# Lightning attention and a highway FFN: three early loads issued from ACT's queue instead of SP's

## The chip, the cores and the metric

The kernel runs as one program on one core of a Trainium2 chip. The metric is the device time of one execution in microseconds (us), and a kernel's time is the median of its runs.

The engines are named as the profile names them: PE (matrix multiply), DVE (vector), ACT (scalar, activations), POOL (GpSimd) and SP, which in this kernel only issues DMAs. A DMA is issued by an instruction in the queue of an engine, in that engine's order. "SPq" and "ACTq" in the profile are such instructions.

## The reference

Inputs are q, k and v of shape (4, 8, 768, 64), that is batch, heads, tokens and head size, a decay `lam` per head, two 512x512 weights and a bias. All are float32.

```python
for b in range(nb):                       # blocks of 64 tokens
    intra = einsum(qb, kb) * Dmask        # Dmask[i,j] = lam**(i-j) for i >= j, else 0
    intra = einsum(intra, vb)
    inter = einsum(qb * lam_pow, kv_state)
    out[:, :, sl] = intra + inter
    kv_state = lam_block * kv_state + einsum(kb * rev_pow, vb)
x = out as (3072 tokens, 512)
H = relu(x @ w_h);  T = sigmoid(x @ w_t + b_t)
result = T * H + (1 - T) * x
```

## The kernel before

**Tiling.** The 4 batches of 768 tokens are cut into 12 steps of 256 tokens, numbered n = 0 to 11, three steps to a batch. Within a step there are two sub-blocks of 128 tokens. The decay is folded into the operands: queries are multiplied by powers of `lam` and values by the inverse powers, so that the state is a plain sum over a batch and the mask is one triangle. Keys are only cast to bfloat16.

**A written-out order.** Each engine runs its instructions in the order of the string `PLAN` (lines 17 to 64). Each word is one piece of work: a name, indices, `@` an engine where there is a choice, and `=` the buffer slots that it opens. The words that matter here, with n the step and p the half of the heads (0: heads 0 to 3, 1: heads 4 to 7, 2: all):

- `Lk.n.p`, `Lq.n.p`, `Lv.n.p` (line 179): load 256 KB of keys, queries or values as 128 partitions x 4 heads x 512 B. `W.w.g` (line 185) loads half of a weight, 512 KB.
- `CK`, `CQ`, `CV` (lines 193 to 207): cast the keys, scale the queries, scale the values, into bfloat16 tiles `kb`, `qb`, `vs`. `WC` (line 189) casts a part of a weight.
- `TK`, `TQ` (line 212): PE transposes. `EK`, `EQ` (line 219): copies of the transposes to SBUF, `kq`.
- `SA.n`, `SB.n` (lines 258 and 263): PE's scores of a step and the updates of its state. `KE` copies the state. `M.n.e.u` (line 278): DVE multiplies 128x512 of scores by the triangle, four times a step.
- `I`, `A`: PE's products with the state and with the values. `D`: copies of the attention's result to `xT`.
- `F.g.u.w` (line 327): PE's FFN products (w = 0: w_h, 1: w_t). `H`, `G`, `X`: DVE's relu, ACT's sigmoid and the product of the two. `R`: PE turns the result back, `E` copies it out, `ST` stores it.
- `Z.r` (line 404): r matrix products of zeros into an unused bank, put where PE would stand idle.
- `LB` (line 389): the powers of the factors, `pow_q` and `pow_v`, on PE, ACT and DVE.

**What sets the order of the loads.** All loads and stores are issued from SP, in the order of `PLAN`. The first ones are `Lv.0.1 Lq.0.1 Lq.0.0 Lk.1.1 Lk.1.0 Lk.0.0 Lk.0.1 Lv.0.0 Lq.1.0 Lv.1.1 Lq.1.1 W.0.1 Lv.1.0 W.0.0`, and then the queries, keys and values of step 2. ACT issues two small DMAs of its own at the very start, `lam` and the bias.

**Semaphores of DMAs.** In the built program the DMAs use eight completion semaphores in turn. A DMA that takes a semaphore which another DMA has used waits, on the engine that issues it, until that other DMA has landed. The first eight DMAs (lam, bias and six loads) wait for nothing.

**The start of the computation.** ACT casts `CK.1.0`, `CK.0.0` and `CK.0.1`, then copies `EK.0.0`, `EK.1.0` and `EK.0.1`. Then PE can do `SA.0`. DVE scales `CQ.0.0`, copies `EQ.0.0` and `EQ.0.1`, scales `CV.0.0` and `CQ.1.0`, and then masks the scores of step 0. POOL does `CV.0.1`, `CK.1.1`, `CQ.0.1`, `CV.1.1`, `CQ.1.1`, parts of the weights, and then the casts of step 2 and later (`CQ.2.2`, `CK.2.2`, `CV.2.2`, ...), each in its order.

Of the kernel before, what the change touches and what calls it, by code (L numbers as in the profile page):

```python
# [8 lines left out]
F32 = mybir.dt.float32  # L9
# [17 lines left out]
F.0.0.0=5 I.1.1=6 Lk.4.0=4 I.1.0=1 Lk.4.1 M.1.1.1=6 M.1.0.1=7 A.1.1 A.1.0 D.1.1@ACT=1 D.1.0@DVE Lv.4.1=4 B=3 Lv.4.0
KE.1.1@DVE=3 BC TQ.2.2=4 EQ.2.2@DVE=2 H.0.1=0 H.0.0=1 Lq.5.0=0 TK.2.2=2 F.1.1.0=1 EK.2.2@ACT CK.3.2@POOL=1 F.1.0.0=6
WC.1.1.0@DVE SA.2=342 SB.2=0 Lq.5.1 WC.1.1.1@ACT F.1.1.1=5 Lk.5.1=0 PT Lk.5.0 M.2.1.1=0 M.2.1.0=3 KE.2.0@ACT=0 I.2.1=2
M.2.0.1=1 G.1.1 Lv.5.0=0 F.0.1.1=4 F.1.0.1=0 G.1.0 Lv.5.1 H.1.1=2 F.0.0.1=1 X.1.1@DVE=0 Lq.6.0=1 I.2.0=5 A.2.1  # L30
M.2.0.0=2 A.2.0 G.0.1 H.1.0=2 X.1.0@DVE X.0.1@DVE=1 D.2.1@DVE=2 R.1=36 TQ.3.2=0 G.0.0 D.2.0@ACT X.0.0@DVE Lk.6.1=1
Lk.6.0 EQ.3.2@DVE=0 Lq.6.1 TK.3.2=4 F.2.1.0=2 CV.3.2@POOL=3 E.1.1@ACT=0 Lq.7.0=2 R.0=56 Lv.6.1=1 EK.3.2@ACT H.2.1=2
SA.3=104 E.0.0@DVE=1 E.0.1@ACT CQ.4.2@POOL=1 F.2.1.1=2 F.2.0.0=6 KE.3.0@ACT=2 I.3.1=5 M.3.1.1=6 SB.3=4 M.3.0.0=7
M.3.1.0=4 Lv.6.0 G.2.1 A.3.0=1 Lq.7.1 E.1.0@ACT KE.3.1@ACT=1 Lk.7.0=2 H.2.0=0 CK.4.2@POOL=0 TK.4.2=0 CV.4.2@POOL=0
EK.4.2@ACT=1 M.3.0.1=5 CQ.5.2@POOL=2 TQ.4.2=3 X.2.1@DVE=0 A.3.1 CK.5.2@POOL=2 F.2.0.1=6 EQ.4.2@DVE I.4.0=4 D.3.0@ACT=1
D.3.1@ACT SA.4=203 M.4.1.0=0 M.4.1.1=1 F.3.0.0=1 F.3.1.0=5 Lk.7.1 CV.5.2@POOL=1 Lv.7.0=2 Lv.7.1 CK.6.2@POOL=1 G.2.0
KE.4.0@ACT=0 SB.4=0 M.4.0.0=2 X.2.0@DVE I.4.1=3 KE.4.1@ACT=3 TK.5.2=2 M.4.0.1=3 TQ.5.2=6 EK.5.2@ACT=2 H.3.1=1
F.3.0.1=0 A.4.0 EQ.5.2@DVE H.3.0=2 SA.5=526 M.5.1.1=4 M.5.0.0=7 CQ.6.2@POOL=0 M.5.1.0=5 A.4.1 G.3.0 D.4.0@ACT=0
F.3.1.1=1 KE.5.0@ACT=2 SB.5=6 M.5.0.1=6 CV.6.2@POOL=2 X.3.0@DVE=1 TK.6.2=4 I.5.0=5 I.5.1=2 A.5.0 A.5.1 D.4.1@ACT G.3.1
D.5.1@ACT D.5.0@DVE R.2=36 E.2.0@DVE=2 Lq.8.1=3 X.3.1@DVE TQ.6.2=0 EQ.6.2@ACT=0 F.4.3.1=5 E.2.1@DVE EK.6.2@ACT G.4.3=0  # L40
F.4.3.0=2 H.4.3=0 F.4.1.1=3 CK.7.2@ACT=0 Lq.8.0 R.3=10 E.3.1@DVE=3 SA.6=642 M.6.1.0=0 Lk.8.1=3 Lk.9.1=4 M.6.0.0=2
CQ.7.2@POOL=1 F.4.1.0=5 H.4.1=1 TQ.7.2=0 M.6.1.1=1 KE.6.0@ACT=1 E.3.0@ACT SB.6=4 Lk.8.0 EQ.7.2@ACT=1 Lk.9.0 G.4.1=1
I.6.1=1 TK.7.2=6 M.6.0.1=3 F.4.2.1=5 EK.7.2@DVE F.4.0.0=0 X.4.3@POOL=0 KE.6.1@DVE=0 G.4.2 A.6.1=2 H.4.0=2
CV.7.2@POOL=3 SA.7=346 KE.7.0@ACT=3 A.6.0 D.6.1@ACT=1 F.4.2.0=0 D.6.0@ACT M.7.1.0=5 M.7.1.1=7 CQ.8.2@POOL=2
CK.8.2@POOL=2 SB.7=4 KE.7.1@ACT=2 Lv.8.0=3 Lv.8.1 H.4.2=3 TQ.8.2=1 TK.8.2=6 M.7.0.1=4 M.7.0.0=6 EQ.8.2@DVE=2 X.4.2@DVE
EK.8.2@ACT X.4.1@POOL F.4.0.1=2 Lq.9.1=4 Lq.9.0 I.7.0=0 G.4.0 Lk.10.0=0 Lv.9.1=4 CK.9.2@POOL=1 TK.9.2=4 EK.9.2@ACT=0
X.4.0@DVE I.7.1=3 A.7.0 A.7.1 D.7.1@ACT Lv.9.0 D.7.0@DVE Lk.11.0=1 Lq.10.1=0 Lq.10.0 CV.8.2@POOL=0 Lk.10.1 ST.1
SA.8=615 M.8.1.1=1 KE.8.0@DVE=1 R.5=24 F.5.0.0=0 E.5.1@DVE=4 M.8.1.0=3 CQ.9.2@POOL=0 TQ.9.2=3 Lv.10.0=0 F.5.3.1=5
F.5.3.0=4 H.5.0=0 E.5.0@ACT CV.9.2@POOL=1 EQ.9.2@ACT SA.9=213 M.8.0.0=0 G.5.3=2 H.5.3=1 SB.8=0 M.9.1.1=2
CQ.10.2@POOL=1 R.4=56 M.9.0.0=5 Lk.11.1 KE.9.0@ACT=0 SB.9=4 Lv.10.1 F.5.1.0=3 KE.9.1@DVE=3 F.5.2.1=2 Lq.11.1=1  # L50
M.8.0.1=6 E.4.0@ACT=0 E.4.1@ACT CK.10.2@ACT=0 I.8.0=5 I.9.1=6 G.5.2 ST.3 Lv.11.1=1 Lq.11.0 M.9.0.1=4 H.5.1=3 M.9.1.0=7
F.5.2.0=0 H.5.2=2 TQ.10.2=4 EQ.10.2@ACT=1 F.5.1.1=3 G.5.1=0 CV.10.2@POOL=2 CK.11.2@POOL=2 X.5.3@POOL=1 ST.5 X.5.2@DVE
ST.4 I.8.1=1 TK.10.2=0 Lv.11.0 EK.10.2@DVE A.9.1=2 A.9.0 D.9.0@ACT=0 D.9.1@DVE A.8.1 A.8.0 SA.10=430 D.8.0@ACT
I.10.0=6 F.5.0.1=2 G.5.0 D.8.1@DVE M.10.1.1=2 M.10.1.0=4 M.10.0.0=5 F.6.2.0=5 F.6.3.1=1 X.5.0@DVE KE.10.0@DVE=2
TK.11.2=0 CQ.11.2@POOL=2 H.6.2=2 F.6.0.0=3 H.6.0=1 EK.11.2@ACT=0 TQ.11.2=4 X.5.1@POOL R.6=25 G.6.3=1 E.6.1@ACT=3
EQ.11.2@ACT E.6.0@ACT R.7=03 E.7.0@DVE=4 E.7.1@DVE SB.10=1 CV.11.2@POOL=3 F.6.3.0=5 M.10.0.1=7 H.6.3=0 KE.10.1@ACT=0
I.10.1=0 F.6.1.0=4 A.10.0 SA.11=321 H.6.1=3 A.10.1 D.10.1@ACT=0 X.6.3@POOL=0 D.10.0@ACT M.11.1.1=1 KE.11.0@DVE=1
M.11.1.0=6 SB.11=5 M.11.0.1=0 F.6.1.1=4 I.11.0=1 ST.0 G.6.1=2 F.6.0.1=0 G.6.0 I.11.1=6 F.6.2.1=2 G.6.2 X.6.0@DVE
F.7.1.0=4 M.11.0.0=3 X.6.2@DVE F.7.1.1=5 G.7.1 H.7.1=0 ST.7 ST.6 ST.2 A.11.1 A.11.0 X.6.1@POOL R.9=03 D.11.1@DVE=0
R.8=24 F.7.0.1=6 E.8.1@ACT=0 F.7.0.0=4 E.9.0@DVE=1 X.7.1@DVE=0 E.9.1@DVE ST.9 E.8.0@DVE ST.8 F.9.0.0=0 D.11.0@ACT=1  # L60
F.9.0.1=5 H.7.0=2 F.8.0.1=1 F.8.0.0=3 F.8.1.1=2 G.7.0 G.9.0 X.7.0@DVE H.9.0=0 R.10=46 G.8.0 H.8.0=1 X.9.0@DVE=0
X.8.0@DVE=1 F.8.1.0=0 H.8.1=2 G.8.1 E.10.1@ACT=4 F.9.1.1=3 R.11.1.0=5 E.10.0@ACT ST.10 F.9.1.0=1 G.9.1 X.8.1@DVE
R.11.0.2=6 E.11.1.0@DVE=0 E.11.0.2@ACT=0 ST.11.1.0 ST.11.0.2 H.9.1=0 X.9.1@DVE R.11.1.1=0 E.11.1.1@DVE=1 ST.11.1.1
"""

GROUPS = [
# [15 lines left out]
def kernel(  # L82
# [11 lines left out]
    nc = tc.nc  # L94
    B, H, S, D = q.shape
    C = 128
# [4 lines left out]
    J = 2  # L101
# [7 lines left out]
    V, A, P, T = nc.vector, nc.scalar, nc.gpsimd, nc.tensor  # L109
# [50 lines left out]
    def new(key, shape, dtype=BF16, tag=None):  # L160
        if key not in made:
            tag = tag or key[0]
            made[key] = sb.tile(shape, dtype, tag=f"{tag}_{slots.pop(0)}", name=tag, bufs=1)
        return made[key]
# [9 lines left out]
    def heads(p):  # L174
        return slice(0, H) if p == 2 else slice(4 * p, 4 * p + 4)


    SRC = {"k": k, "q": q, "v": v}
    def load(x, n, p):
        b, c = divmod(n, NST)  # L180
        hs = heads(p)
        nc.sync.dma_start(out=new((x + "f", n), [128, H, J * D], F32)[:, hs],  # L182
                          in_=SRC[x][b, hs, c * 2 * C:(c + 1) * 2 * C, :].rearrange("h (p j) d -> p h (j d)", j=J))

    def load_w(w, g):
        nc.sync.dma_start(out=w_f[w][:, :, 256 * g:256 * g + 256],  # L186
                          in_=(moe_w_h, moe_w_t)[w][:, 256 * g:256 * g + 256].rearrange("(kc p) m -> p kc m", p=128))

    def cast_w(w, g, i, eng):
        at = slice(2 * i, 2 * i + 2), slice(256 * g, 256 * g + 256)  # L190
        copy(eng, w_b[w][:, at[0], at[1]], w_f[w][:, at[0], at[1]])
# [212 lines left out]
    def spin(r, idle=[0]):  # L404
# [3 lines left out]
            T.matmul(t, lhsT=blank[:, 0:128], rhs=blank, start=True, stop=True)  # L408

    DO = {  # L410
        "Lk": lambda a, e: load("k", *a), "Lq": lambda a, e: load("q", *a), "Lv": lambda a, e: load("v", *a),
        "W": lambda a, e: load_w(*a), "WC": lambda a, e: cast_w(*a, e),
        "CK": lambda a, e: cast_k(*a, e), "CQ": lambda a, e: cast_q(*a, e), "CV": lambda a, e: cast_v(*a, e),
        "TK": lambda a, e: trans("k", *a), "TQ": lambda a, e: trans("q", *a), "T": lambda a, e: trans_both(*a),
# [11 lines left out]
    for token in PLAN.split():  # L426
        token, _, at = token.partition("=")
        token, _, eng = token.partition("@")
# [34 lines left out]
```

## Time and profile before

| | |
|---|---|
| median of 6 runs | 106.54 us (105.66 to 107.8) |
| profiled execution, its own time | 107.03 us |
| its span, first to last instruction | 105.3 us |
| granted PE clock | 1.000 |
| busy: PE, PE's weight loads, DVE, ACT, POOL | 96.8, 69.1, 81.8, 68.6, 61.3 us |
| DMA | 27.57 MB, mean 262 GB/s |

The profile comes from one execution. Its own time lies 1.7 us above its span, and 0.49 us above the median of the runs. A line of the timeline gives start and duration in us, engine, source line, operation and tiles; in brackets stands the engine's idle time before it and what ended that.

### The profile page before, as it was taken

To read this page: it belongs to the slowest core of one execution; us is meant where nothing else is said; L and a number is where in the kernel's file an instruction comes from. 1 tells how busy PE (TensorE), PEld (TensorE's weight loads), DVE (VectorE), ACT (ScalarE), POOL (GpSimd) and SP (SyncE) were. 2 spreads that over 40 slices of the span, in tenths; PEclk is the share of its full clock that TensorE was granted. 3 is DMA by queue.
4 is the path that set the end of the run, shared out by engine and by line. 5 is a ranking of instruction groups with operands and counts; after the bars stand their busy time and mean duration, and the time that the engine had idled before them with its cause. 6 is when DMAs were issued, how large, how long until landed. Compare 5 with 4: busy or idle time off the path is not lost.

```text
span 105.3 us, 4744 instructions
## 1 busy us (share of the span) xinstructions
PE 96.8 (92%) x2075; PEld 69.1 (66%) x2086; DVE 81.8 (78%) x139; ACT 68.6 (65%) x116; POOL 61.3 (58%) x53
## 2 busy tenths in 40 slices
PE   6979989969999999999999999999999999999940
PEld 2325555848887888888657568564685756789930
DVE  3021782968999995989869999999789699799860
ACT  3306759427869699488897589645862867557940
POOL 6423180397477989739899699924699613400000
PEclk9999999999999999999999999999999999999999
DMA  1999999999999999999999999999999029303773
GB/s 51 270 318 290 307 327 308 239 294 305 301 294 287 279 304 282 306 293 278 284 299 306 271 289 285 308 335 324 304 341 364 15 106 375 123 6 121 276 264 142
DMA packets 43582, 27.57 MB, mean 262 GB/s; under 512 B 1446, under 2 KB 40618, under 8 KB 43562
## 3 DMA queue, kind: packets, MB, share of 16 engines
q1 hardware_dynamic: 43552, 27.27, 89.3%
q8 instruction: 16, 0.26, 1.0%
q14 instruction: 4, 0.03, 0.1%
q10 hardware_dynamic: 10, 0.00, 0.0%
HBM read 20.97 MB, written 6.29 MB: 259 GB/s over the span
## 4 chain that ended last, share of the span: by engine, by line
PE 60%; SPq 23%; DMA 6%; DVE 2%; issue 2%; POOL 2%; ACT 0%; DVEq 0%; ACTq 0%; POOLq 0%
SPq L182 20%; PE bt L331 16%; PE bh L331 16%; DMA vf<-in_v_dram 6%; PE bs L237 5%; PE bo L305 5%; PE bx L375 5%; PE bqtr L217 4%; PE bktr L217 4%; PE bo L294 3%; SPq L186 3%; PE kv L242 3%; POOL vs L200 2%; DVE th L345 1%; DVE hm L335 1%
## 5 line engine op out<-in xcount | busy, mean ns | idle before, releaser
L279 DVE TENSOR_TENSOR m<-bs,tri 128x512 bf16<-128x512 f32 x48 | 30.8, 683 | 4.5 <-PE bs L237 3.2
L331 PEld LDWEIGHTS <-w_b 128*128 128x128 bf16 x320 | 27.0, 98 | 10.3
L200 POOL TENSOR_TENSOR vs<-vf,pow_v 128x1024 bf16<-128x1024 f32 (+1 forms) x12 | 21.1, 1758 | 9.6 <-DMA vf<-in_v_dram 8.3
L331 PE MATMUL bh<-xT,w_b 128*128 128x256 bf16 (+2 forms) x155 | 24.4, 292 | 0.5
L331 PE MATMUL bt<-xT,w_b 128*128 128x256 bf16 (+2 forms) x156 | 24.3, 292 | 0.2
L200 POOL TENSOR_TENSOR qb<-qf,pow_q 128x1024 bf16<-128x1024 f32 (+1 forms) x12 | 21.1, 1759 | 4.7 <-DMA qf<-in_q_dram 4.7
L342 ACT ACTIVATE bt<-bt,bt_col 128x256 f32<-128x256 f32 (+2 forms) x34 | 15.5, 462 | 6.5 <-PE bt L331 4.6
L335 DVE SCALAR_TENSOR_TENSOR hm<-bh,xT 128x512 bf16<-128x512 f32 (+1 forms) x26 | 16.6, 644 | 2.1 <-PE bh L331 1.2
L117 ACT ACTIVATE xT<-bo 128x512 bf16<-128x512 f32 x17 | 12.1, 749 | 4.7 <-PE bo L305 4.6
L345 DVE TENSOR_TENSOR th<-bt,hm 128x512 bf16<-128x512 f32 (+1 forms) x20 | 12.4, 631 | 1.4 <-ACT bt L342 0.8
L117 ACT ACTIVATE kq<-bktr 128x1024 bf16<-128x1024 bf16 (+1 forms) x12 | 10.3, 877 | 3.7 <-PE bktr L217 3.5
L237 PE MATMUL bs<-kq 64*64 64x128 bf16 x384 | 12.5, 218 | 0.0
L119 POOL CAST kb<-kf 128x1024 bf16<-128x1024 f32 (+1 forms) x9 | 8.9, 989 | 4.8 <-DMA kf<-in_k_dram 2.3
L117 ACT ACTIVATE ss<-kv 128x512 bf16<-128x512 f32 x14 | 8.4, 599 | 3.6 <-PE kv L242 3.4
L237 PEld LDWEIGHTS <-kq 64*64 64x64 bf16 x384 | 9.1, 107 | 1.9 <-issue 1.5
L345 POOL TENSOR_TENSOR th<-tb,hm 128x512 bf16<-128x512 f32 x6 | 6.9, 1158 | 4.8 <-DVE hm L335 3.1
L408 PE MATMUL bspin<-blank 128*128 128x512 bf16 x30 | 9.4, 459 | 0.2 <-issue 0.2
L117 ACT ACTIVATE o<-bx 128x512 f32<-128x512 f32 x12 | 6.9, 596 | 3.8 <-DMA out_dram<-o 2.0
L242 PE MATMUL kv<-vs,kb 64*64 64x64 bf16 x320 | 9.0, 195 | 0.3
L217 PE MATMUL bktr<-id,kb 128*128 128x128 bf16 x96 | 7.5, 220 | 1.3 <-POOL kb L119 1.1
L217 PE MATMUL bqtr<-id,qb 128*128 128x128 bf16 x96 | 7.7, 220 | 0.9 <-POOL qb L200 0.9
L242 PEld LDWEIGHTS <-kb 64*64 64x64 bf16 x320 | 7.0, 108 | 1.9 <-issue 1.5
(56 smaller groups left out, 125.2 us busy)
## 6 DMA issues: line engine op xcount, KB each, us to landing
vf<-in_v_dram SPq DMA_DIRECT2D x24, 256.0 KB, 5.6
qf<-in_q_dram SPq DMA_DIRECT2D x24, 256.0 KB, 5.4
kf<-in_k_dram SPq DMA_DIRECT2D x24, 256.0 KB, 5.5
out_dram<-o SPq DMA_DIRECT2D x11, 512.0 KB, 5.3
w_f<-in_moe_w_h_dram SPq DMA_DIRECT2D x2, 512.0 KB, 7.1
w_f<-in_moe_w_t_dram SPq DMA_DIRECT2D x2, 512.0 KB, 5.7
out_dram<-oh SPq DMA_DIRECT2D x2, 128.0 KB, 2.1
out_dram<-oq SPq DMA_DIRECT2D x1, 256.0 KB
```

Source lines behind the costliest of these rows:

```text
L117: A.activation(dst, src, AF.Copy)
L182: nc.sync.dma_start(out=new((x + "f", n), [128, H, J * D], F32)[:, hs], in_=SRC[x][b, hs, c * 2 * C:(c + 1) * 2 * C, :].rearrange("h (p j) ...
L200: ENG[eng].tensor_tensor(dst, in0=get(src, n)[:, heads(p)].rearrange("p h (j d) -> p h j d", j=J), in1=pw[:, n % NST, heads(p), :, None].t ...
L217: T.transpose(t[:, i, j, :], get(x + "b", n)[:, j, h:h + 2, :], id128)
L237: T.matmul(get("s", n, e, hp // 2)[half(b), hp % 2, j, :], lhsT=kq(n)[half(e), 0, hp, j, half(b)], rhs=kq(n)[half(e), 1, hp, :, half(b)], ...
L242: T.matmul(kv[half(e), hp, half(e)], lhsT=get("kb", n)[half(b), j, 2 * hp + e, :], rhs=get("vs", n)[half(b), 2 * hp + e, j, :], start=firs ...
L279: V.tensor_tensor(new(("m", n, e, u), [128, 2, J, C]), in0=get("s", n, e, u), in1=tri[:, None].to_broadcast([128, 2, J, C]), op=ALU.mult)
L331: T.matmul(t[:, r, :], lhsT=w_b[w][:, kc, m * 128:(m + 1) * 128], rhs=xT(g)[:, kc, :], start=(kc == 0), stop=(kc == KC - 1))
L335: V.scalar_tensor_tensor(new(("hm", g, u), [128, len(rows(g, u)), size(g) * C], tag=f"hm{size(g)}"), in0=get("h", g, u), scalar=0.0, in1=x ...
L342: A.activation(get("tt", g, u)[:, r, :], t[:, r, :], AF.Sigmoid, bias=bt_col[:, m:m + 1])
L345: ENG[eng].tensor_tensor(new(("th", g), [128, NP, size(g) * C], tag=f"th{size(g)}")[:, span(g, u), :], in0=get("tt", g, u), in1=get("hm", ...
L408: T.matmul(t, lhsT=blank[:, 0:128], rhs=blank, start=True, stop=True)
```

## The change

Three loads move from SP's queue to ACT's: the keys of step 1, heads 0 to 3 (`Lk.1.0`), the keys of step 0, heads 4 to 7 (`Lk.0.1`), and the queries of step 1, heads 0 to 3 (`Lq.1.0`). On ACT they stand behind the last of the powers (`pow_v`) and ahead of `CK.1.0`. The rest of `PLAN`, and so the order of every other instruction on every engine, is the same. The function `load` takes the engine; every source line after it is one higher.

```diff
-Lv.0.1=0 CV.0.1@POOL=0 Lq.0.1=0 Lq.0.0 Lk.1.1=0 CQ.0.0@DVE=0 CK.1.1@POOL=0 TK.1.1=0 TQ.0.0=1 CQ.0.1@POOL Lk.1.0
-CK.1.0@ACT Lk.0.0=1 CK.0.0@ACT=1 Lk.0.1 Z.5=2 TK.0.0=2 Lv.0.0 Lq.1.0=1 Lv.1.1=1 CV.1.1@POOL=1 TK.1.0=3 TQ.0.1=4
+Y.3=0 LB=6 Z.11=0 Lv.0.1=0 CV.0.1@POOL=0 Lq.0.1=0 Lq.0.0 Lk.1.1=0 Lk.1.0@ACT Lk.0.1@ACT=1 Lq.1.0@ACT=1 CQ.0.0@DVE=0
+CK.1.1@POOL=0 TK.1.1=0 TQ.0.0=1 CQ.0.1@POOL CK.1.0@ACT Lk.0.0 CK.0.0@ACT=1 Z.5=2 TK.0.0=2 Lv.0.0 Lv.1.1=1
...
-    def load(x, n, p):
+    def load(x, n, p, eng):
         b, c = divmod(n, NST)
         hs = heads(p)
-        nc.sync.dma_start(out=new((x + "f", n), [128, H, J * D], F32)[:, hs],
+        (A if eng == "ACT" else nc.sync).dma_start(
+            out=new((x + "f", n), [128, H, J * D], F32)[:, hs],
...
-        "Lk": lambda a, e: load("k", *a), "Lq": lambda a, e: load("q", *a), "Lv": lambda a, e: load("v", *a),
+        "Lk": lambda a, e: load("k", *a, e), "Lq": lambda a, e: load("q", *a, e), "Lv": lambda a, e: load("v", *a, e),
```

The semaphores are dealt out anew with the change. In the built program, the start of the two queues and what each DMA waits for is then:

```
ACT: lam, bias, powers (LB),
     Lk.1.0   waits until Lq.0.0 has landed
     Lk.0.1   waits until Lk.0.0 has landed
     Lq.1.0   waits until Lv.0.0 has landed
     CK.1.0, CK.0.0, CK.0.1, EK.0.0, EK.1.0, EK.0.1, ...
SP:  Lv.0.1, Lq.0.1, Lq.0.0, Lk.1.1, Lk.0.0, Lv.0.0   wait for nothing
     Lv.1.1 (lam), Lq.1.1 (Lv.0.1), W.0.1 (bias), Lv.1.0 (Lq.0.1), W.0.0 (Lk.1.1),
     Lq.2.0 (Lv.1.1), Lq.2.1 (Lq.1.1), Lk.2.1 (W.0.1), Lk.2.0 (Lv.1.0), Lv.2.1 (Lk.1.0),
     Lv.2.0 (W.0.0), W.1.1 (Lk.0.1), W.1.0 (Lq.1.0), ...
     in brackets: whose landing it waits for
```

## The prediction

> **What bounds the kernel now.** I read the page first (PE 92% busy, the chain that ended last 60% PE, 23% SP's queue, 6% DMA), then the chain in order of time, to see where the loads hand over to PE:
>
> ```profile
> 26.70 6.33 DMA vf<-in_v_dram
> 33.16 1.91 POOL vs L200
> 35.08 0.04 issue
> 35.12 0.22 PE kv L242 x2
> ```
>
> To 33.03 us the chain is the stream of loads, one behind the other. The values of step 3 land, POOL scales them, and PE starts SA.3 at 35.12. PE had waited only 0.15 us there, so PE's own chain ended at 34.97: two chains end together, and either alone can move the end later. From there PE is the bound, as the busy times by stretch show (stretch, length, PE's busy us):
>
> ```profile
> 40.00:60.00 20.00, 19.84 (x505) 14.75 (x505) 17.25 (x29) 15.52 (x26) 16.64 (x12) 1.00 1.08 291
> 60.00:80.00 20.00, 19.60 (x454) 13.17 (x453) 18.69 (x31) 14.13 (x21) 15.71 (x11) 1.00 1.04 313
> 80.00:99.00 19.00, 18.89 (x430) 14.28 (x430) 16.81 (x29) 12.37 (x25) 5.77 (x5) 1.00 0.46 168
> ```
>
> PE is idle 0.16 + 0.40 + 0.11 = 0.67 us in 59, in small pieces. What is late at 35.12 comes out at the end almost whole.
>
> The timeline of the start:
>
> ```profile
> 1.30 1.04 SPq L182 DMA_DIRECT2D qf<-in_q_dram  x2
> 2.38 2.99 SPq L182 DMA_DIRECT2D kf<-in_k_dram  x4
> 3.54 0.23 ACT L396 ACTIVATE pow_v<-p_ln 128x48 f32<-128x48 f32 x1
> 6.48 0.69 DVE L200 TENSOR_TENSOR qb<-qf,pow_q 128x512 bf16<-128x512 f32 x1 [3.12 <-DMA qf<-in_q_dram]
> 7.33 0.61 POOL L119 CAST kb<-kf 128x512 bf16<-128x512 f32 x1 [2.34 <-DMA kf<-in_k_dram]
> 8.15 0.83 SPq L182 DMA_DIRECT2D qf<-in_q_dram  x1
> 8.22 0.63 ACT L117 ACTIVATE kb<-kf 128x512 bf16<-128x512 f32 x1 [4.45 <-DMA kf<-in_k_dram]
> 9.10 0.63 ACT L117 ACTIVATE kb<-kf 128x512 bf16<-128x512 f32 x1 [0.26 <-DMA kf<-in_k_dram]
> 10.00 0.63 ACT L117 ACTIVATE kb<-kf 128x512 bf16<-128x512 f32 x1 [0.27 <-DMA kf<-in_k_dram]
> 10.54 1.55 ACT L117 ACTIVATE kq<-bktr 128x512 bf16<-128x512 bf16 x3
> ```
>
> The reader should see the landings here, as the starts of instructions that waited for one: Lq.0.0 by 6.4, Lk.1.1 7.3, Lk.1.0 8.2, Lk.0.0 9.1, Lk.0.1 10.0. They come 0.88 us apart. SP had issued all of them by 5.37 us (the first at some 0.5 us each): the DMAs' pace limits here, not the issuing. The three casts of ACT and its three copies follow the landings without slack; PE's SA.0 starts at 12.09, when the copies are out. Behind it (DVE, then PE):
>
> ```profile
> 12.96 2.48 DVE L279 TENSOR_TENSOR m<-bs,tri 128x512 bf16<-128x512 f32 x4 [0.45 <-PE bs L237]
> 21.93 0.73 DVE L119 CAST xT<-bo 128x512 bf16<-128x512 f32 x1 [1.05 <-PE bo L305]
> 25.09 0.85 DVE L119 CAST w_b<-w_f 128x512 bf16<-128x512 f32 x1
> 26.58 1.89 DVE L279 TENSOR_TENSOR m<-bs,tri 128x512 bf16<-128x512 f32 x3 [0.65 <-PE bs L237]
> ```
>
> ```profile
> 26.72 1.05 PE L331 MATMUL bt<-xT,w_b 128*128 128x256 bf16 x8
> 31.91 0.20 PE L375 MATMUL bx<-id,th 64*128 64x64 bf16 x2 [0.20 <-DVE th L345]
> ```
>
> **The change part by part.**
>
> *Issues taken off SP.* SP saves three issues of 0.5 to 0.83 us. I cost that at nothing: a load's landing is set by the 0.88 us of transfers ahead of it. Were this cover gone, SP would stand some 2 us further ahead, which buys no byte. Later SP issues do get later: Lk.2.1 now waits for W.0.1 (POOL casts it at 15.15; issued at 13.60 before), Lk.2.0 for Lv.1.0 (16.01 against 14.87). Still queued then are W.0.0 (512 KB) and two to three loads, over 3 us of transfers at 0.88, against the 3.0 us that a load took at least (shortest issue to landing in the view of vf). Cost nothing; at most the 1.5 us of delay, on keys cast at 22.51, when POOL has only just finished the queries.
>
> *Waits brought to ACT.* ACT is done with the powers at 3.77 and would sit idle until 8.22. Now its first issue waits for Lq.0.0, so 6.45 to 6.95. The second waits for Lk.0.0, which moves up into the slot of 8.2 and shares its end with the first ACT load: 8.5. The third waits for Lv.0.0, which moves into the slot of 9.1 and shares with Lk.1.0: between 9.1 and its old 10.9, I take 9.8, and 0.5 for the issue: 10.3. Queued behind these waits on ACT are CK.1.0, CK.0.0, CK.0.1 and everything after. CK.1.0, data or not, starts at 10.35 instead of 8.22, CK.0.0 at 10.9.
>
> *The price of a load on ACT's queue.* No row of before shows one of this size. Bounds: 3.0 us from issue to landing with nothing ahead, and 5.5 us, the median of vf issues behind a full SP queue. Its own queue holds nothing ahead of it, so the first row is nearer; with half of one 0.88 us transfer for sharing I take 3.4. Lk.0.1 then lands at 8.5 + 3.4 = 11.9; the bounds give 8.25 + 3.0 = 11.25 and 8.5 + 5.5 = 14.0. It landed at 10.0. So CK.0.1, the three copies and SA.0 come 1.9 us later (1.25 to 4.0): SA.0 at 14.0. Lq.1.0 lands at 9.8 + 3.4 = 13.2, and DVE has scaled it by 13.9, ahead of the scores at 14.85: hidden, and at the upper bound too (15.3 + 0.7 = 16.0 against 16.95).
>
> The Trainium skill, "DMA: Bandwidth & Descriptors", section "Issuing engines are not separate DMA queues", says that DMAs from several engines run on the same 16 DMA engines and interleave, and that a second issuing engine saves only issue time. The 0.88 us spacing behind issues of 0.5 us agrees. Taken alone the rule would make the sum zero, since it doesn't speak of waits ahead of an issue; the waits above make the loss.
>
> *What of 1.9 us reaches the end.* Scores, masks, products and the blank matmuls of step 0 follow SA.0 in one chain, and so do those of step 1: DVE's copy at 21.93 waited for PE's bo and moves by 1.9 too. From there DVE is dense to 25.94, the end of its weight cast. F.1.1.1 on PE needs this weight and started at 26.72, so 0.78 us is absorbed: 1.9 - 0.78 = 1.12. PE's waits at 22.62 and 23.60 for POOL (0.58 and 0.36) vanish on the way; they can't save more, as DVE is the later one. DVE's masks at 26.58 had 0.65 of slack and move by 1.25; they fill about 0.2 in two small gaps, so th at 31.91 is late by 1.05 and takes R.1 with it, 1.04. At 35.12, 0.15 is absorbed: 0.9. After that I take 0.1 of the 0.67: 0.8 us in all. Late next is DVE, dense from 26.58 to 40, and the chain of loads no longer decides at 35.12.
>
> The profiled execution is 107.03, its span 105.3, and becomes 107.8. It lies 0.49 above the median, so the median goes from 106.54 to 107.3 (+0.75%). The same sum at the lower bound: 1.25 - 0.78 - 0.15 - 0.1 = 0.2, so 106.8; at the upper: 4.0 - 1.13 = 2.9, so 109.4.
>
> **The rivals.**
>
> *Nearly all absorbed.* ACT's queue gets its share at once, a load takes 3.0 us, and the bubbles at 26.58, 31.91 and 35.12 eat the rest: 0 to +0.3 us, 106.5 to 106.8. For it: the bubbles are there. Against it: two loads at a time can hardly each be as quick as one alone.
>
> *ACT's loads wait like SP's.* If a load on ACT comes behind what SP has outstanding, it takes 4.5 to 5.5 us, SA.0 moves 3.0 to 4.0, and the end 1.8 to 2.9: 108.3 to 109.4. For it: SP has five to seven loads queued at that time. Against it: these loads stand in another queue.
>
> *Faster.* With two queues the DMAs could carry more than one load in 0.88 us. It decides only if SA.0 doesn't slip, that is if Lv.0.0 lands before some 7.7 (8.22 less the issue of 0.5) instead of 9.1 at best; three loads overlapped would bring the stream forward by up to 2.6 us, but PE can give back no more than its waits of 0.58, 0.36, 0.20 and 0.15: 1.3 us, 105.25. Against it: the even spacing.
>
> *The moved issues start at once behind the powers, as the change reads, and the waits cost nothing.* Then Lk.1.0 goes out at 3.8. Against it: Lq.0.0 is not there before 6.4. It would fall among the absorbed or the faster case.
>
> **How the numbers follow.** Forecast, 106.8 to 108.3, likeliest 107.3: 0.46. Nearly all absorbed: 0.24. Like SP's: 0.22. Faster: 0.08. A measurement of this kernel can tell about 1% from no change, here 1.07 us, so slower begins at 107.6: all of the case like SP's (0.22) and 0.20 of the forecast's 0.46, together 0.42. Faster by over 1%, below 105.5: 0.06 of the last case. Within: 0.52. The range from 106.2 to 108.9 leaves out most of the faster case (0.07) and the upper half of the case like SP's (0.11).
>
> **What would show it.** In the changed profile: ACT's three issues at about 6.4, 8.5 and 9.8; its first cast of keys at 10.3, the third at 11.9; SA.0 at 14.0; DVE's weight cast ending at 27.8 and F.1.1.1 with it; POOL's vs of step 3 still at 33.2; SA.3 at 36.0 with no wait for POOL. The forecast is wrong if the third issue is through before 8.5, if Lk.0.1 lands outside 11.25 to 14.0, if PE still waits for POOL at 22.62 or 35.12, or if the load stream itself shifts at 33.0.

## The result, and the profile after

The changed kernel takes 113.52 us (median of 22 runs, 111.64 to 114.71) against 106.27 (46 runs, 105.23 to 108.16) of the kernel before: ratio 1.058, 95% interval 1.054 to 1.061. The prediction was 107.3, its range 106.2 to 108.9. Ratios here leave out slow runs, those over 1.5% above the fastest of their kernel (13 of these 22), while medians don't; the profiled execution shown first, 114.12 us with a span of 112.3, is such a run, as are those of e5 (110.73) and e12 (113.84), so its start is read here and the second profile (e8, span 110.7) stands beside it where the end matters. The ratio of the two medians is 1.068.

The timeline of the start after the change (start and duration in us, engine, line, operation, tiles; in brackets the idle time before it and what ended that):

```profile
6.35 2.33 ACTq L182 DMA_DIRECT2D kf<-in_k_dram  x2
6.43 0.65 SPq L187 DMA_DIRECT2D w_f<-in_moe_w_h_dram  x1
7.12 1.08 SPq L182 DMA_DIRECT2D vf<-in_v_dram  x1
8.24 0.80 SPq L187 DMA_DIRECT2D w_f<-in_moe_w_h_dram  x1
9.07 0.38 ACTq L182 DMA_DIRECT2D qf<-in_q_dram  x1
12.26 1.15 ACT L117 ACTIVATE kb<-kf 128x512 bf16<-128x512 f32 x2 [8.50 <-DMA kf<-in_k_dram]
13.46 0.69 PE L218 MATMUL bktr<-id,kb 128*128 128x128 bf16 x8 [3.76 <-ACT kb L117]
16.08 0.63 ACT L117 ACTIVATE kb<-kf 128x512 bf16<-128x512 f32 x1 [2.67 <-DMA kf<-in_k_dram]
16.77 0.61 PE L218 MATMUL bktr<-id,kb 128*128 128x128 bf16 x4 [2.18 <-ACT kb L117]
18.01 0.69 DVE L201 TENSOR_TENSOR qb<-qf,pow_q 128x512 bf16<-128x512 f32 x1 [2.37 <-DMA qf<-in_q_dram]
20.73 2.48 DVE L280 TENSOR_TENSOR m<-bs,tri 128x512 bf16<-128x512 f32 x4 [2.02 <-PE bs L238]
```

The page's list of DMA issues (count, KB each, median us from issue to landing) has two rows for ACT's queue:

```profile
kf<-in_k_dram ACTq DMA_DIRECT2D x2, 256.0 KB, 6.9
qf<-in_q_dram ACTq DMA_DIRECT2D x1, 256.0 KB, 8.9
```

The issues come nearly when the prediction said, at 6.35, 8.21 and 9.07, and nothing lands when it said. The casts that wait for the keys start at 12.26 (8.22 before) and 16.08 (10.00 before), and the first mask of scores at 20.73 (12.96 before). The chain that ended last goes through just these loads (start, us, what):

```profile
2.92 5.28 DMA kf<-in_k_dram
8.19 0.02 issue
8.21 7.84 DMA kf<-in_k_dram
16.06 0.02 issue
16.08 0.64 ACT kb L117
```

This is Lk.0.0, which the second issue waits for, and then Lk.0.1, 7.84 us from issue to landing. Where these went is seen when all loads are put in the order of their issue, from whichever queue (times read from the trace's records of issues and completions):

```
             issued   landed              issued   landed
Lk.0.0         2.92     8.19    Lv.1.0      7.12    14.74
Lv.0.0         3.47     9.04    Lk.0.1 ACT  8.21    16.06
Lv.1.1         4.29     9.94    W.0.0       8.24    17.17
Lq.1.1         5.54    11.32    Lq.1.0 ACT  9.07    17.99
Lk.1.0 ACT     6.35    12.24    Lq.2.0      9.95    18.33
W.0.1          6.43    13.24    Lq.2.1     11.34    19.24
```

The order of the landings is the order of the issues, over both queues. And SP runs ahead: W.0.1 goes out at 6.43 instead of 9.03, Lv.1.0 at 7.12 instead of 9.90, W.0.0 at 8.24 instead of 10.78. Between its issue and its landing, Lk.0.1 had Lv.0.0, Lv.1.1, Lq.1.1, Lk.1.0, W.0.1 (twice the size) and Lv.1.0 to wait for: seven units of 256 KB and its own, eight in 7.85 us, 0.98 each. In the kernel before it stood in front of all of them but Lk.1.0.

While PE waits 3.76 and 2.18 us, its granted clock (the share of the full clock that it is given) falls (stretch, length, busy us of PE, PE's weight loads, DVE, ACT and POOL, then the clock, the DMAs' share and GB/s):

```profile
12.00:14.00 2.00, 0.54 (x9) 0.54 (x10) 0.00 (x0) 1.15 (x2) 1.04 (x2) 0.97 1.16 309
14.00:16.00 2.00, 0.58 (x6) 0.32 (x3) 1.02 (x2) 0.00 (x0) 0.00 (x0) 0.50 1.14 320
16.00:18.00 2.00, 1.23 (x6) 0.70 (x7) 0.00 (x0) 1.92 (x4) 0.61 (x1) 0.50 1.20 295
18.00:20.00 2.00, 1.64 (x31) 0.86 (x34) 0.69 (x1) 0.17 (x1) 0.63 (x1) 0.50 1.20 290
20.00:22.00 2.00, 2.00 (x58) 1.21 (x51) 1.27 (x3) 0.60 (x1) 2.00 (x2) 0.82 1.18 303
```

The DMAs never rest meanwhile (290 to 320 GB/s): the bytes come as fast as before, in another order. Behind the start, the places at which the prediction had seen slack (DVE, then POOL, of the kernel after):

```profile
32.61 1.57 DVE L119 CAST w_b<-w_f 128x512 bf16<-128x512 f32 x1
34.10 1.87 DVE L280 TENSOR_TENSOR m<-bs,tri 128x512 bf16<-128x512 f32 x3
```

```profile
32.00 1.90 POOL L201 TENSOR_TENSOR vs<-vf,pow_v 128x1024 bf16<-128x1024 f32 x1
```

The masks of step 2 are 7.52 us late (26.58 before). POOL's values of step 3 are there 1.2 us earlier than before: the stream of loads, the other chain that ended at 35, has become quicker and no longer matters.

Two theories stood after this. **A: the order of issue.** The DMAs serve loads in the order in which they are issued, whatever the queue; the waits make ACT's three loads late in that order, and SP, with three issues fewer, puts other bytes in front. **B: ACT's queue.** A load from ACT's queue is slower by itself, served behind or beside SP's. Both left open how much of the loss is the fallen clock (e3, e4, e8 to e10).

### The profile page after: what moved, and what is told of

Same layout as the page of the kernel before. It is cut to its first block, busy times and chain, and to the rows that moved or that the text cites. A ratio compares the mean times of both kernels' runs of the same rounds, so it can differ in the third digit from the quotient of the medians.

```text
span 112.3 us, 4744 instructions
## 1 busy us (share of the span) xinstructions
PE 97.9 (87%) x2075; PEld 70.0 (62%) x2086; DVE 83.5 (74%) x139; ACT 68.7 (61%) x116; POOL 61.5 (55%) x53
## 4 chain that ended last, share of the span: by engine, by line
PE 68%; DMA 12%; DVE 11%; issue 3%; SPq 2%; ACT 2%; DVEq 0%
PE bh L332 17%; PE bt L332 15%; DMA kf<-in_k_dram 12%; PE bs L238 6%; PE bo L306 6%; PE bx L376 5%; PE bktr L218 4%; DVE m L280 4%; PE bqtr L218 4%; PE bo L295 4%; PE kv L243 3%; PE bspin L409 3%; DVE hm L336 2%; DVE th L346 2%; SPq L182 2%
## 5 line engine op out<-in xcount | busy, mean ns | idle before, releaser
L218 PEld LDWEIGHTS <-kb 128*128 128x128 bf16 x96 | 5.9, 99 | 8.4 <-ACT kb L117 6.7
L117 ACT ACTIVATE kb<-kf 128x512 bf16<-128x512 f32 (+1 forms) x5 | 3.9, 799 | 11.2 <-DMA kf<-in_k_dram 11.2
L409 PE MATMUL bspin<-blank 128*128 128x512 bf16 x30 | 10.5, 500 | 0.2 <-issue 0.2
L119 DVE COPY kq<-bqtr 128x1024 bf16<-128x1024 bf16 (+1 forms) x7 | 4.3, 608 | 7.1 <-PE bqtr L218 7.1
```

What stands on the lines that cost most here:

```text
L117: A.activation(dst, src, AF.Copy)
L119: ENG[eng].tensor_copy(dst, src)
L218: T.transpose(t[:, i, j, :], get(x + "b", n)[:, j, h:h + 2, :], id128)
```

## The experiments

The table gathers all runs. Delays are against the profile of the kernel before (first mask 12.96, masks of step 2 26.58). "Waits" is the sum (us) of PE's waits of over 0.3 us between 40 and 100 us for which the profile names nothing that ended them. "End" is the ratio less 1, times the median of before (106.27 to 106.82).

| kernel | Lk.0.1 landed | first mask | masks of step 2 | waits | end | median us | ratio, interval |
|---|---|---|---|---|---|---|---|
| after | 16.06 | +7.77 | +7.52 | none | +6.1 | 113.52 | 1.058, 1.054 to 1.061 |
| e1 early issue | 10.56 | +3.11 | +1.72 | none | +1.3 | 107.49 | 1.012, 1.001 to 1.022 |
| e2 all on SP | 16.39 | +8.10 | +6.83 | none | +5.9 | 113.19 | 1.055, 1.039 to 1.072 |
| e3 PE kept busy | 15.62 | +5.93 | +5.44 | 1.0 | +6.4 | 112.89 | 1.060, 1.050 to 1.071 |
| e4 early, busy | 10.53 | +1.00 | +0.35 | 0.8 | +0.6 | 107.36 | 1.006, 1.001 to 1.010 |
| e5 only Lk.0.1 | 12.91 | +3.66 | +3.44 | 0.9 | +1.1 | 109.37 | 1.010, 1.005 to 1.015 |
| e6 only Lk.1.0 | 9.23 | +5.70 | +4.72 | none | +4.8 | 111.06 | 1.046, 1.040 to 1.051 |
| e7 only Lq.1.0 | 9.77 | +0.22 | -0.04 | none | +0.2 | 106.78 | 1.002, 0.999 to 1.006 |
| e8 after, again | 15.59 | +7.30 | +6.49 | none | +6.0 | 112.57 | 1.056, 1.048 to 1.064 |
| e9 as e3, again | 15.40 | +5.72 | +4.68 | 1.7 | +6.1 | 112.80 | 1.057, 1.050 to 1.064 |
| e10 as e5, busy | 13.03 | +3.05 | +1.68 | 0.8 | +1.8 | 108.25 | 1.017, 1.010 to 1.024 |
| e11 scores late | 10.14 | +2.10 | +1.35 | 0.4 | +0.6 | 107.49 | 1.006, 1.001 to 1.011 |
| e12 scores late | 10.22 | +6.07 | +4.96 | 2.2 | +5.7 | 112.91 | 1.054, 1.047 to 1.061 |

The delay of step 2's masks foretells the end in every kernel without such waits: the end is from 0.2 above to 0.9 below it (after's own profile is 1.4 off). The waits occur in all six kernels that have more blank matmuls, and in e5, and in none of the other seven, the kernel before among them; ahead of 40 us e7 has one of 0.43 us, at 38.33.

What PE waits for in them can be read from the trace's records. A queue that the page calls "instruction" (q8) carries 16 transfers of 16 KB in a run, some 5 us apart, against some 4160 matmuls and weight loads of PE: one transfer for each 260 of them. All twelve waits, e7's among them, end 1.36 to 1.60 us after the end of such a transfer. And they stand at five places only, counted in PE's instructions: 1214, 1470, 1726, 2745 and 3257 (within one), that is 256 or a multiple of it apart, short of five between the third and the fourth (a trace can lack some records). This says that PE had run out of instructions there and waited for the next block. Added blank matmuls, about two instructions each, change which work stands at these places, but e5 and e7 have such waits with none added. No run varied this alone.

**e1: the same three loads on ACT's queue, but issued early.** They stand ahead of the powers' exponentials, where they wait for no other load.

```diff
+    def early(at):
+        if at == 1:
+            slots[:] = [0, 1, 1]
+            load("k", 1, 0, "ACT")
+            load("k", 0, 1, "ACT")
+            load("q", 1, 0, "ACT")
...
         A.activation(ln_bc, t, AF.Ln)
+        early(1)
...
         A.activation(pow_q, p_ln, AF.Exp)
```

> The three loads stay on ACT's queue, but are issued one instruction earlier group-wise: behind the logarithm and ahead of the two exponentials of the powers (about 3.1, 3.6 and 4.1 us instead of 6.35, 8.21 and 9.07). The semaphores are then dealt out so that they wait only for the landings of lam and the bias, which are long there. Theory A (the loads of both queues are served in the order in which they were issued, and the loss comes from the waits ahead of ACT's issues): Lk.1.0 lands at 9.1, Lk.0.1 at 10.0, Lq.1.0 at 11.8, SA.0 starts at about 12.3, the PE clock stays at 1.0, and the time is that of the kernel before, 106.3 (105.8 to 107.0). Rival B (ACT's queue itself is served badly beside a full SP queue): 6 to 9 us from issue to landing as in the changed kernel, Lk.0.1 at 11.5 or later, SA.0 at 14 or later, time 108 or more.

The timeline of e1:

```profile
2.84 0.45 ACTq L182 DMA_DIRECT2D kf<-in_k_dram  x1
3.34 0.52 ACTq L182 DMA_DIRECT2D kf<-in_k_dram  x1
3.94 0.48 ACTq L182 DMA_DIRECT2D qf<-in_q_dram  x1
8.28 0.63 ACT L117 ACTIVATE kb<-kf 128x512 bf16<-128x512 f32 x1 [3.44 <-DMA kf<-in_k_dram]
9.24 0.61 PE L218 MATMUL bktr<-id,kb 128*128 128x128 bf16 x4 [2.51 <-POOL kb L119]
10.24 1.15 ACT L117 ACTIVATE kb<-kf 128x512 bf16<-128x512 f32 x2 [1.32 <-DMA kf<-in_k_dram]
```

From the same queue the keys now land at 8.26 and 10.56, nearly as early as from SP before (8.20 and 9.98). So most of the loss is not the queue's. The time, 107.49, lies between the two forecasts, and the clock did not stay up. What is left, 1.2%, goes with sharing among neighbours: the loads that the two queues issue in turn land in pairs (8.26 and 8.52, 10.21 and 10.56, 12.02 and 12.37). Lk.1.1 on SP, issued 0.46 us ahead of ACT's first load, landed 0.26 us behind it and 1.25 later than before, so PE stood idle for 2.51 us ahead of 9.24, and its clock fell to 0.50 in 10 to 12 us.

**e2: no load on ACT; all on SP, in the order of issue that the changed kernel's trace shows.**

```diff
-Lv.0.1=0 ... Lk.1.1=0 Lk.1.0@ACT Lk.0.1@ACT=1 Lq.1.0@ACT=1 ... Lk.0.0 ... Lv.0.0 Lv.1.1=1 ... Lq.1.1 ... W.0.1 Lv.1.0 ... W.0.0
+Lv.0.1=0 Lq.0.1=0 Lq.0.0 Lk.1.1=0 Lk.0.0=1 Lv.0.0 Lv.1.1=1 Lq.1.1=1 Lk.1.0 W.0.1 Lv.1.0 Lk.0.1 W.0.0 Lq.1.0
```

> All loads on SP, no load on ACT, but in the order in which the two queues of the changed kernel issued them: Lk.1.0 behind Lq.1.1, Lk.0.1 behind W.0.1 and Lv.1.0, Lq.1.0 behind W.0.0. Theory A: the landings are those of the changed kernel within 1 us (Lk.0.1 at 15.1 to 16.1, Lk.1.0 at 11.8 to 12.2), PE stands idle over 3 us before 13.4 again and its granted clock falls, and the time is 112 to 114. Rival B: without ACT's queue the three loads come 2 us or more earlier, the clock holds, and the time is 107 to 110.

```profile
7.18 0.73 SPq L182 DMA_DIRECT2D kf<-in_k_dram  x1
9.81 0.82 SPq L182 DMA_DIRECT2D kf<-in_k_dram  x1
12.15 1.15 ACT L117 ACTIVATE kb<-kf 128x512 bf16<-128x512 f32 x2 [8.39 <-DMA kf<-in_k_dram]
16.41 0.63 ACT L117 ACTIVATE kb<-kf 128x512 bf16<-128x512 f32 x1 [3.11 <-DMA kf<-in_k_dram]
```

Without any of the three on ACT the casts wait until 12.15 and 16.41 (12.26 and 16.08 in the changed kernel), and the time is the same within its interval, 113.19. Theory B falls as the cause of this loss: the order is enough to make it.

**e3 and e9: the changed kernel with PE kept busy in its two gaps.** 24 blank matmuls instead of 5 ahead of the first transposes that wait, ten more ahead of the second.

```diff
-CK.0.0@ACT=1 Z.5=2 TK.0.0=2 ... TQ.0.1=4 EQ.0.0@DVE=0
+CK.0.0@ACT=1 Z.24=2 TK.0.0=2 ... TQ.0.1=4 Z.10=6 EQ.0.0@DVE=0
```

> The changed kernel with more blank matmuls where PE stood idle: 24 instead of 5 ahead of TK.0.0, and 10 new ones ahead of TK.0.1. No load moves. If the fall of the granted clock to 0.50 from about 13 to 21 us costs what the trace suggests (SA.0 18.2 instead of 19.4, the first mask 19.0 instead of 20.7), the clock stays at 1.0 and the time falls by 1.3 to 1.7 us, to 111.8 to 112.2: most of the loss stays. Rival C (the clock is most of the loss): 107 to 109. Rival D (the clock is worth nothing, as DVE and ACT limit there): 113.2 to 113.8.

The clock stayed at 1.00 (mean 0.997), the first mask came 1.84 us earlier, and the time, 112.89, was hardly other than after's. The pair was run again side by side on one chip:

> The changed kernel once more, unaltered, to stand beside the next run on the same chip. All theories: 113 to 114, as in its own runs; PE idle for 3.8 us and then 2.2 us before the keys' transposes, and the granted clock at 0.50 for some 7 us from 13.5 on.

> The changed kernel with blank matmuls in PE's two gaps (as in e3_kept_busy), beside the unaltered one on the same chip. If the clock's fall is a separate cost of its own: faster than e8_after_again by 0.5 to 1.5 us, clock 0.99 or above. If the clock's fall costs nothing, because the wait for the loads decides anyhow: the same within 0.3 us. Nobody expects the loss of 7 us to go: the keys land just as late.

112.57 (a little under the 113 to 114 expected of e8) and 112.80: no gain, which is what had been set down for a fall of the clock that costs nothing. The profiles say more. The DVE timeline of e8, then that of e9, and PE's of e9:

```profile
20.26 2.48 DVE L280 TENSOR_TENSOR m<-bs,tri 128x512 bf16<-128x512 f32 x4 [1.86 <-PE bs L238]
32.68 0.46 DVE L119 CAST w_b<-w_f 128x512 bf16<-128x512 f32 x1
33.07 1.89 DVE L280 TENSOR_TENSOR m<-bs,tri 128x512 bf16<-128x512 f32 x3
```

```profile
18.68 2.48 DVE L280 TENSOR_TENSOR m<-bs,tri 128x512 bf16<-128x512 f32 x4 [0.36 <-PE bs L238]
31.26 1.87 DVE L280 TENSOR_TENSOR m<-bs,tri 128x512 bf16<-128x512 f32 x3
```

```profile
72.75 0.38 PE L218 MATMUL bqtr<-id,qb 128*128 128x128 bf16 x4 [1.27 <-issue]
83.60 0.31 PE L238 MATMUL bs<-kq 64*64 64x128 bf16 x8 [0.47 <-issue]
```

The clock of e9 where e8's falls to 0.67 and 0.50:

```profile
14.00:16.00 2.00, 1.95 (x16) 1.06 (x15) 1.02 (x2) 0.57 (x2) 0.00 (x0) 1.00 1.12 321
```

With the clock kept up, the start is 1.6 to 1.8 us ahead (18.68 against 20.26, 31.26 against 33.07), and a mask at 72.91 still stands 1.75 ahead of its like at 74.66. Not all of this is the clock: Lk.0.1 landed 0.19 us earlier in e9 than in e8, and 0.44 earlier in e3 than in the first profile after. Less that, both pairs give 1.4 us at the first mask. Then PE waits 1.27 and 0.47 us in e9, "issue" in the profile, for the blocks of instructions described above; e8 has no such waits, and at the end the two are level within 0.3 us. PE's busy time says the same (e9, then e8):

```profile
72.00:92.00 20.00, 18.62 (x401) 11.99 (x403) 16.57 (x27) 12.59 (x18) 10.77 (x8) 1.00 0.50 163
```

```profile
72.00:92.00 20.00, 19.79 (x436) 12.91 (x440) 18.38 (x31) 13.20 (x19) 12.55 (x9) 1.00 0.52 169
```

So the fallen clock is worth some 1.4 us at the start, but in the kernels that keep it up by blank matmuls waits of PE take the gain back. Where it is lost is shown; that the blank matmuls bring these waits is only suggested by the table.

**e4: e1 with PE kept busy** (21 blank matmuls instead of 11 ahead of the first transposes).

```diff
-Y.3=0 LB=6 Z.11=0 Lv.0.1=0
+Y.3=0 LB=6 Z.21=0 Lv.0.1=0
```

> The kernel without waits on ACT (three loads on ACT's queue, issued behind the logarithm), with 21 instead of 11 blank matmuls ahead of TK.1.1. There PE stood idle 2.51 us before 9.24 and its granted clock fell to 0.50 until about 12.5. Theory A (what was left of the loss there, 0.9 us, is the clock and not ACT's queue): the clock holds at 1.0, the scores of step 0 start at 12.2 to 12.8 instead of 14.75, and the time is 105.9 to 106.8, not to be told from the kernel before. Rival B (a load on ACT's queue costs in itself): 107 or more, with the clock at 1.0.

The clock stays up, the first mask comes at 13.96, 2.1 us before e1's, and the ratio is 1.006, within e1's wide interval. The median, 107.36, missed the 105.9 to 106.8 of theory A and fell where the rival had been put. The landings speak against the rival: ACT's keys landed 0.2 and 0.55 us later than before (8.43 and 10.53), SP's own Lk.1.1 and Lk.0.0 1.3 and 1.1 (8.55 and 10.19, for 7.27 and 9.08). With these neighbours late, the first mask still lags by 1.0 us. A cost of some 0.6% from having loads on two queues at once remains possible.

**e5, e6, e7: one load on ACT at a time**, behind the powers as in the change, the other two on SP as before.

```diff
-Lk.1.1=0 Lk.1.0@ACT Lk.0.1@ACT=1 Lq.1.0@ACT=1
+Lk.1.1=0 Lk.0.1@ACT=1        (e5)
+Lk.1.1=0 Lk.1.0@ACT          (e6)
+Lk.1.1=0 Lq.1.0@ACT=1        (e7)
```

> Only Lk.0.1 moves to ACT's queue; in this program its issue waits until Lk.1.1 has landed (7.3 us). Theory A (served in the order of issue): SP has issued ten loads by then, so it lands as the eleventh, at about 13.5 instead of 10.0; PE stands idle some 3 us before TK.0.1 (12.9 to 14.1), SA.0 starts at 15.7 and the time is 109 to 110.5, the upper end if the clock falls. Rival (a load alone on ACT's queue takes 3.0 to 3.4 us, as I had forecast): it lands at 10.7, and the time is 106.3 to 106.8.

> Only Lk.1.0 moves to ACT's queue; its issue waits until Lk.1.1 has landed (7.3 us). Theory A: it lands as the eleventh, at about 13.5 instead of 8.2, and holds the first of ACT's three casts of keys and all behind it: SA.0 at about 16.7, PE idle some 5 us before, so that the clock falls: 110 to 112. Rival (3.0 to 3.4 us on ACT's queue): lands at 10.7, SA.0 at 13.9, the time 107 to 107.5.

> Only Lq.1.0 moves to ACT's queue; its issue waits until Lk.1.1 has landed (7.3 us). Theory A: it lands as the eleventh, at about 13.5 instead of 11.8; DVE scales it ahead of the masks of step 0, which start at 14.2 instead of 13.0; later waits take up 0.8 of it, and the time is 106.3 to 107.2. Nothing waits on ACT, as its first cast comes at 8.2 anyway and the issue is over by 7.8. Rival (any load on ACT costs by itself, through ACT or through the transfers): 107.5 or more.

The issues and the casts that wait for them, e5, e6 and e7 in turn:

```profile
7.51 0.40 ACTq L182 DMA_DIRECT2D kf<-in_k_dram  x1
12.93 0.63 ACT L117 ACTIVATE kb<-kf 128x512 bf16<-128x512 f32 x1 [2.98 <-DMA kf<-in_k_dram]
```

```profile
7.56 0.40 ACTq L182 DMA_DIRECT2D kf<-in_k_dram  x1
12.85 1.67 ACT L117 ACTIVATE kb<-kf 128x512 bf16<-128x512 f32 x3 [9.08 <-DMA kf<-in_k_dram]
18.66 1.89 DVE L280 TENSOR_TENSOR m<-bs,tri 128x512 bf16<-128x512 f32 x3 [1.48 <-PE bs L238]
```

```profile
7.09 0.40 ACTq L182 DMA_DIRECT2D qf<-in_q_dram  x1
12.51 0.74 DVE L201 TENSOR_TENSOR qb<-qf,pow_q 128x512 bf16<-128x512 f32 x1 [1.03 <-DMA qf<-in_q_dram]
```

All three loads take 5.3 to 5.4 us, on the scale of SP's in the kernel before (medians 5.4 to 5.6 by its page). Only the place in what follows differs. Lq.1.0 is needed late, and no loss clear of noise is seen. Lk.0.1 is the last key load anyway: 2.9 us late. Its nine runs fall into two groups, four at 107.09 to 107.54, of which the ratio of 1.010 is made, and five at 109.37 to 111.72, to which the profile belongs. Lk.1.0 is the dear one, 4.6%, though its keys belong to step 1: its cast stands first in ACT's order, so the casts of Lk.0.0 and Lk.0.1, which had landed at 8.45 and 9.23, wait behind it, and all three run at 12.85. In e6 it landed at 12.83, ahead of Lq.1.1 (13.70), which had been issued 0.25 us before it: neighbours in the order can swap. The same swap is in e5, e7 and e10 (0.20 to 0.24 us), and halves of a weight were passed in e3 and e8 (0.01 to 0.09). In all of these SP's issuing instruction began first and ended last (in e6, 7.31 to 8.44 against ACT's 7.56 to 7.96), so by the ends of the issues the order of landing holds there. In e1 and e4 it does not: there Lk.1.0 landed ahead of Lk.1.1 though SP's issue ended first (2.89 against 3.29 in e1).

**e10: e5 with ten blank matmuls in PE's gap**, to see whether the clock makes e5's spread.

```diff
-TK.1.0=3 TQ.0.1=4 EQ.0.0@DVE=0
+TK.1.0=3 TQ.0.1=4 Z.10=6 EQ.0.0@DVE=0
```

> Only Lk.0.1 on ACT's queue, with ten blank matmuls in PE's gap of 2.8 us ahead of its transposes. In e5_only_k01 the runs fell into two groups, 107.1 to 107.5 and 109.4 to 111.7, with clocks of 0.99 and 0.96 to 0.98. If the fallen clock makes the second group: all runs at 107.0 to 107.8 and clock at 0.99 or above. If the two groups have another cause, such as the loads: both groups again, median near 109.

Neither held. The clock stayed at 0.99 or above in all runs and the spread shrank from 4.6 to 2.0 us (107.73 to 109.69), but the runs at 107.1 to 107.5 were gone too; the ratio is 1.017. The two intervals (1.005 to 1.015 and 1.010 to 1.024) overlap. Not settled.

**e11 and e12: the kernel before, loads untouched, with PE's first scores made late by blank matmuls directly ahead of them.** This takes the prediction's other step by itself: what a delay at SA.0 does to the end.

```diff
-Z.5=1 SA.0=612
+Z.14=1 SA.0=612       (e11)
+Z.32=1 SA.0=612       (e12)
```

> The kernel before with nine more blank matmuls on PE directly ahead of SA.0 (14 instead of 5): all loads as before, SA.0 and everything behind it some 1.85 us later (nine by 0.22, less 0.14 of slack). This is the prediction's step on what of 1.9 us reaches the end, by itself. If it holds: 1.85 - 1.13 = 0.7 us, ratio 1.007. If a delay there passes through whole: 1.85 us, ratio 1.017.

> The same with 27 more blank matmuls (32 instead of 5): SA.0 some 5.8 us later, nearly as late as in the changed kernel (7.3), with the loads and the clock as before. If the late scores alone make the loss and about 1.1 us are absorbed: 4.7 us, ratio 1.044. Passed through whole: 5.8, ratio 1.054. If the changed kernel's loss comes from its order of loads in another way than through the late scores, this is much below: under 3 us.

DVE's masks of steps 0 and 2 in e11, then of e12 the blank matmuls, the first products and two waits further on:

```profile
15.06 2.48 DVE L279 TENSOR_TENSOR m<-bs,tri 128x512 bf16<-128x512 f32 x4 [2.40 <-PE bs L237]
27.93 1.87 DVE L279 TENSOR_TENSOR m<-bs,tri 128x512 bf16<-128x512 f32 x3
```

```profile
11.17 7.07 PE L408 MATMUL bspin<-blank 128*128 128x512 bf16 x31
18.17 0.22 PE L242 MATMUL kv<-vs,kb 64*64 64x64 bf16 x2
42.42 0.81 PE L331 MATMUL bh<-xT,w_b 128*128 128x256 bf16 x6 [0.72 <-issue]
47.80 0.30 PE L237 MATMUL bs<-kq 64*64 64x128 bf16 x6 [0.67 <-issue]
```

e11: 2.10 us late at the first mask, 1.35 late at the masks of step 2, 0.6% late at the end (0.1 to 1.1%). The step holds at its own size. e12: 6.07 us late at the first mask, 4.96 at step 2, where 1.1 us are absorbed. The end, 1.054 or +5.7, is the number set down for a delay passed through whole, and above the 4.7 for 1.1 us absorbed. The profile speaks for the second: the masks are 4.82 us late just before the first of the waits of 0.72, 0.67 and 0.82 us, and the span is 6.8 longer at the end. With the loads and the clock of the kernel before, late scores bring nearly the changed kernel's time (112.91), but 2.2 us of that are waits which the changed kernel doesn't have. Less these, scores 6.07 us late cost some 4.6 us of span; e8's, 7.30 late and without such waits, cost 5.4. By this reckoning the late scores explain the loss. Taking the waits off one for one is argued, not shown.

## Why the prediction was wrong

**"Waits brought to ACT": right.** The three waits were read from the built program, and the issues came at 6.35, 8.21 and 9.07 for 6.45, 8.5 and 9.8. The rival in which they start at once behind the powers falls.

**"The price of a load on ACT's queue": the step that failed.** It took 3.4 us, between 3.0 and 5.5; measured were 5.9, 7.85 and 8.9. The reason given was "Its own queue holds nothing ahead of it". What counts is not what stands ahead in the queue but what has been issued before by anybody: e2 gives the same landings with no load on ACT. The rows for it stood in the trace of before: Lk.0.1, issued by SP at 4.15, landed at 9.98, 5.8 us later, with five loads ahead of it. The lower end, 3.0, is what the first load of all takes (0.80 to 3.77), with nothing ahead of it; the upper, the median of vf, is 5.6 and not 5.5 in its view.

The Trainium skill, "DMA: Bandwidth & Descriptors", section "Queues, rings and completion order", says that each DMA engine takes turns, packet by packet, between the queues that have work. Read by itself, this would let a load on an otherwise empty ACT queue overtake the loads that SP has waiting. None of the three did in the changed kernel's profile; where page and measurement differ, the measurement decides. The pairs of e1, 0.26 to 0.35 us apart, are what taking turns between neighbours would look like. The section that the prediction cited, that a second issuing engine is not a second set of DMA engines, agrees with e2.

**"Issues taken off SP" at nothing, "which buys no byte": failed too.** SP did stand further ahead, by 2.5 to 2.8 us at W.0.1, Lv.1.0 and W.0.0. It bought no byte, but it set these bytes in front of ACT's second and third load: W.0.1 and Lv.1.0 are three of the seven units that Lk.0.1 waited for, 2.9 us at 0.98. An earlier issue is not free where the order of issues is the order of service. Nor did SP's later issues get later: Lk.2.1 went out at 13.26 for 13.60, as W.0.1, which it waits for, had itself been issued earlier.

**"What of 1.9 us reaches the end": right for its size.** e11 puts 2.1 us on SA.0 and gets 0.6% at the end (0.8 us were forecast for 1.9), with the delay, still 2.05 at the start of the weight cast, shrinking to 1.35 at the masks of step 2 behind it, where the prediction had put it. (Its three sums take off 1.1, 1.03 and 1.13 us, which decides nothing.) In e8 the same place brings 7.59 us (masks of step 1, 25.98 for 18.39) down to 6.49. In the profile first shown it absorbs only 0.27 of 7.79, as the weight cast lasted 1.57 us instead of 0.85.

**The missing term: PE's clock.** The prediction had no line for it. Two gaps of 3.76 and 2.18 us bring 0.50 for some 7 us, and the scores some 1.4 us more delay (e8 and e9, e3 and after), a fifth of the 7.3. Nearly all of the rest is the landings: Lk.0.1 came 5.6 us later in e8 than before. How much of the 1.4 reaches the end was not seen.

**The rivals.** "ACT's loads wait like SP's" (0.22) named the right mechanism, "behind what SP has outstanding", and priced it at 4.5 to 5.5 us from SP's rows; that SP would meanwhile run ahead makes it up to 8.9. It gave 108.3 to 109.4. The head of ACT's order was in the text ("queued behind these waits on ACT are CK.1.0, CK.0.0, CK.0.1") and is what e6 shows to be the dearest of the three moves.

**What stays open.** Whether added blank matmuls bring PE's waits for instructions (0.4 to 1.3 us each); no run here took the waits away by themselves. So a changed kernel with its clock kept up and no such waits, up to 1.4 us quicker by this reckoning, was not seen. The 0.6% of e4 and the spread of e5's runs are not settled either.

## What to carry to other kernels

Moving a load to another queue moves its place in the order of all issues, and that place, at the 0.9 us that each 256 KB ahead of it takes here, sets its landing; so look at who else will be issued earlier because of the move. A load that reuses the semaphore of another load (here there are eight in turn) is issued only when that one has landed, and what stands behind it on its engine waits with it: price the engine's order, not only the load. An issue placed ahead of the waits (e1) costs a fifth of one placed behind them (1.2% against 5.8%), and it still gained nothing over SP alone.

## What the runs showed of the hardware that was not expected

- Loads from two engines' queues land in the order of issue over both, except that neighbours issued 0.01 to 0.47 us apart swapped (e1, e3 to e8, e10). Behind the powers every swap fits the order in which the issuing instructions ended; in e1 and e4, where the queues alternate, loads land in pairs.
- PE seems to run out of instructions at times: twelve waits of 0.37 to 1.27 us stand at steps of 256 of its instructions and end 1.36 to 1.60 us after a 16 KB transfer of the queue "instruction".
- PE's granted clock fell to 0.50 after idle gaps of 2.51 us (e1), 2.77 (e5) and 3.76 (after). The Trainium skill, "TensorE: Matmul & The Clock Gate", section "What's actually happening", puts an idle window of about 3.4 us ahead of a fall; here shorter gaps, with little work beside them, were enough.
- The same cast of a weight on DVE, 128x512 from f32 to bf16, took 0.46 us in e8, 0.85 in the kernel before and 1.57 in the first profile after. In the last, POOL's scalings of 128x1024 ran beside all of it; in e8 the scaling began 0.13 us behind the cast's start. That the one slows the other was not tried. Such rows move by 1.1 us between executions of one kernel, so a slack of that size can't be counted on.
